# Mamba-2 SSD and a merged expert layer on one core: a split chunk output, a moved gated product and a reordered last step

## The chip, the cores and the metric

The kernel runs on one core of a Trainium2 chip. The metric is the device time of one execution in microseconds, lower being better. The core has five engines that run side by side, each with its own queue of instructions: TensorE (PE, matrix products into PSUM, with PEld for the loads of its stationary operand), VectorE (DVE), ScalarE (ACT), GpSimd (POOL) and SyncE (SP, which here issues DMAs). All data are float32.

## What is computed

Two stages follow one another. The first is the chunked state-space scan of Mamba-2, for 4 batches of 8 heads over 768 positions, with head size 32 and state size 16. The second is a layer of four experts (256 to 1024 to 256), all of which see every token, weighted by normalised domain probabilities.

```python
# stage 1, per chunk of positions: cum = cumsum(log a)
L = exp(cum[i] - cum[j]) * (i >= j)
y = ((C @ B.T) * L) @ x + (C @ state) * exp(cum)
state = exp(sum(log a)) * state + sum_j(B[j] x[j] * exp(cum[-1] - cum[j]))
# stage 2, tokens as rows of 8 heads x 32 = 256
p = domain_probs / (domain_probs.sum(-1, keepdims=True) + 1e-9)
out = sum_e p[:, e:e+1] * (maximum(x @ w1[e], 0) @ w2[e])
```

## The kernel before, in words

**Tiling.** The 3072 tokens are 24 chunks of 128, and these are 6 blocks (k) of 4 chunks (512 tokens, two halves b1 and b2 of 256). A block's chunks come from the four batches. Per block the second stage takes 8 steps (r), one for each expert e and each half jj of its hidden layer (512 of 1024 units); n counts the 48 steps. From step `PLAIN` = 2 on, each step does its first product (w1) and its second (w2) as seven products of half-size blocks, a Strassen scheme in Winograd's form; the sums of weights are made once by GpSimd (`sums_of`, L178) and kept in DRAM, the sums of activations by DVE (`sums`, `diff`) and in PSUM.

**Order of the work.** It is written out by hand (a manual schedule): the program text is the order of each engine's queue, and an engine waits only where an operand or a buffer isn't ready. The steps of the second stage of one block are interleaved with the first stage of the next block's chunks. Buffers are rotating pools; a tile waits until the readers of the tile that held its slot are done.

**First stage.** `spread` and `decay_part` make the decay factors LT by scans on DVE, `masks` makes the masked C (ACT), `scores` the products C B (PE), `masked` multiplies scores by LT (DVE, L396), and `outputs` (L408) makes y on PE (L430). y lies with the state's new part A in one PSUM tile of pool `ps_att` (tag "att", two buffers). ACT copies it to yT (L439) and A (L443, L444, L446).

**Second stage.** `fmul` (L477) makes the seven first products in two PSUM banks X and Y; `snap` (ACT, L498) copies bank X, `total` (DVE, L503) adds bank Y to a copy and gives z, `gated` (DVE, L513) takes max(z, 0) times the gate and gives h, and `diff` (DVE, L520) makes the sums T of h. `smul` (L561) makes the seven second products, one step later, into the PSUM tiles acc0 to acc3 (L576). The seven have the positions (1, 3, 7, 5, 6, 2, 4) in these: 1 and 3 in acc0, 7 and 5 in acc1, 6 and 2 in acc2, 4 in acc3. `plain_first` (L530) and `plain_second` are the ordinary products that the first two steps use.

**The start.** Chunks 0 to 3 are made one after another while there is no other work. `outputs([1])` (L716) is followed on PE by the first product of step 0 (`plain_first(0, 1, (0,))`, L540), which reads yT of chunks 0 and 1.

**A step with scores** (r = 3 and 6 in all blocks but the last, ten in all): after `gated(n, "21", "X")` comes `gated(n, "12", "z12")` (L847), then `smul(n - 1, 6)`, `scores` and the eight masked products (L853), then the T differences.

**The end.** For the first five blocks, `combine` and `turned_out` (a transpose on DVE in blocks of 32x32) prepare the result, and `leave` (L667) issues it from SP in pieces of 32 partitions, 16 KB each, over later steps. The last block has no later step: `finish` (L609) does the seven second products of the last step, the sums u and o, transposes on PE (L627), copies and three DMAs of 256, 128 and 128 KB (L651, L656, L658).

Of the kernel before, what the change touches and what calls it, by code (L numbers as in the profile page):

```python
# [8 lines left out]
FP32 = mybir.dt.float32  # L9
# [3 lines left out]
P = 128  # L13
NQ, NT = 4, 2
# [3 lines left out]
def kernel(  # L18
# [38 lines left out]
    nc = tc.nc  # L57

    NCH, _, W = xbc.shape
    E, DM, F = w1.shape  # L60
# [329 lines left out]
    def masked(cs, rs):  # L390
        for r in rs:
            for c in cs:
                q = r ^ 2 * turned_round(c)
                h = slice(NT * q, NT * q + NT)
                s = st[c]
                nc.vector.tensor_mul(s["MT"][:, h, 0:P], s["g"][q], s["LT"][:, h])  # L396
# [8 lines left out]

    state = {}

    def outputs(cs):  # L408

        ys = {}  # L410
# [119 lines left out]
    def plain_first(n, b, a=(0, 1)):  # L530

        k = n // SPB
        cols = slice(b * HB - HB, b * HB)
        f = first.setdefault(n, {})
        for bank, ws in [(("X", (A11, A12)), ("Y", (S3, A22)))[i] for i in a]:
            pool, tag = (ps_f, bank) if n or b > 1 else (ps_s, {"X": "acc2", "Y": "acc3"}[bank])
            f[bank] = pool.tile([P, JJ, HB], FP32, tag=tag, name=bank)
            for j in range(JJ):
                for i, w in enumerate(ws):
                    nc.tensor.matmul(  # L540
                        out=f[bank][:, j], lhsT=wt1[n][:, w, j * P:j * P + P],
                        rhs=yT[k][:, i, cols], start=(i == 0 and j == 0), stop=(i == 1),
                        skip_group_check=True)
# [39 lines left out]
    def keep(k, u):  # L583
        e = kept[k, u] = ffn.tile([P, 2, HB], FP32, tag=f"kept{u}", name=f"kept{u}", bufs=1)
        nc.scalar.copy(out=e, in_=acc[k, u])
# [23 lines left out]
    def finish(n):  # L609


        k = n // SPB
        add = nc.vector.tensor_add
        b1, b2 = slice(0, HB), slice(HB, BLK)
        o = ffn.tile([P, 2, BLK], FP32, tag="o", name="o", bufs=1)
        u = ffn.tile([P, 3, HB], FP32, tag="u", name="u", bufs=1)
        turned, rows = {}, {}

        def turn_out(b, d):
            if b not in turned:  # L620
                rows[b] = ffn.tile([P, 2, DM], FP32, tag="z", name="rows", bufs=3)
                turned[b] = [ps_f.tile([P, DM], FP32, tag=tag, name="turned") for tag in "XY"] \
                    if b == 0 else ps_att.tile([P, 2, DM], FP32, tag="att", name="turned")
            for i in range(2):
                lo = b * HB + i * P
                t = turned[b][i] if b == 0 else turned[b][:, i]
                nc.tensor.transpose(t[:, d * P:d * P + P], o[:, d, lo:lo + P], ident[:, 0])  # L627

        def dst(b):
            return out.rearrange("(i k p) m -> k p i m", k=NBLK, p=P)[k][:, 2 * b:2 * b + 2]  # L630

        smul(n, 1)
        smul(n, 3)
        keep(k, 0)
        p1, p3 = kept[k, 0][:, 0], kept[k, 0][:, 1]
        smul(n, 6)
        add(u[:, 0], acc[k, 2][:, 0], p1)
        add(u[:, 1], u[:, 0], p3)
        smul(n, 7)
        smul(n, 5)  # L640
        p7, p5 = acc[k, 1][:, 0], acc[k, 1][:, 1]
        add(u[:, 2], p7, u[:, 0])
        add(o[:, 1, b2], p5, u[:, 2])
        add(o[:, 0, b2], p5, u[:, 1])
        smul(n, 2)
        add(o[:, 0, b1], acc[k, 2][:, 1], p1)
        turn_out(1, 1)
        smul(n, 4)
        turn_out(1, 0)
        nc.scalar.copy(out=rows[1], in_=turned[1])  # L650
        nc.sync.dma_start(out=dst(1), in_=rows[1])  # L651
        turn_out(0, 0)
        add(o[:, 1, b1], acc[k, 3][:, 0], u[:, 2])
        turn_out(0, 1)
        nc.vector.tensor_copy(rows[0][:, 0], turned[0][0])
        nc.sync.dma_start(out=dst(0)[:, 0], in_=rows[0][:, 0])  # L656
        nc.scalar.copy(out=rows[0][:, 1], in_=turned[0][1])
        nc.scalar.dma_start(out=dst(0)[:, 1], in_=rows[0][:, 1])  # L658

    def turned_out(k):  # L660

# [2 lines left out]
        ot = kept[k, "ot"] = ffn.tile([P, 2, BLK // 32, 32], FP32, tag="ot", name="ot", bufs=1)  # L664
        nc.vector.transpose(ot.rearrange("p d b j -> p d (b j)"), o)

    def leave(k, c):  # L667

        dst = out.rearrange(
            "(c k b i) (d a j) -> c k a d i b j", k=NBLK, i=32, b=P // 32, j=32, d=2)[c, k]  # L670
        for q in range(P // 32):
            for d in range(2):
                nc.sync.dma_start(
                    out=dst[q, d],
                    in_=kept[k, "ot"][32 * q:32 * q + 32, d, P // 32 * c:P // 32 * (c + 1)])

    def opened(n):

# [34 lines left out]
    masked([1], (0, 1, 2))  # L713
    spread(2, ((ps_s, "acc2"), (ps_s, "acc3"), (ps_f, "Y"), (ps_s, "acc0")))
    masks(2)
    outputs([1])  # L716
    sum_w1(0, 0)
    load_decays(3)
    load_w2(1)
# [54 lines left out]
    for n in range(PLAIN, NS):  # L774
# [69 lines left out]
        total(n, 6, "12")  # L844
        fmul(n, 4)
        gated(n, "21", "X")
        gated(n, "12", "z12")  # L847
        if r == SPB - 1 and k < NBLK - 1:
            sums(k + 1)
        smul(n - 1, 6)  # L850
        if scored:
            scores(scored, ((ps_att, "att"), (ps_att, "att"), (ps_f, "Y"), (ps_f, "X")))
            masked(scored, (3, 2, 0, 1))  # L853
        smul(n - 1, 2)
        diff(n, "T3", "22", "12")
        smul(n - 1, 4)
# [60 lines left out]
```

## Time and profile before

| | |
|---|---|
| median of 4 runs | 639.97 us (639.66 to 640.31) |
| the profiled execution's own time | 640.31 us |
| its span, first to last instruction | 638.5 us |
| PE busy, its idle | 632.9 us (99%), 5.6 us |
| granted TensorE clock | 1.00 of full speed throughout |
| DVE, ACT, POOL busy | 483.8, 119.4, 109.8 us |
| chain that ended last | PE 98% of the span, DVE 1% |
| bytes moved by DMA | 121.61 MB, mean 190 GB/s |
| one second product (4 PE records) | 0.86 us |

In the timeline rows of the profile, the first column is the start in microseconds from the span's start, the second the duration; then come the engine, the source line, the operation, the tiles (output and inputs), and in brackets the idle time just ahead with what ended it. A fp32 matmul of 128x256 shows as two records; "x8" are eight records. The ends of matmuls are modelled: a record lasts some 0.2 us longer than the time until the next can start. Rows on PEld are loads of the stationary operand.

### The profile page before, as it was taken

Reading aid. Unit: us, or ns where it says so; the run is one execution under the profiler, and the core shown is the slowest. Engines: PE = TensorE matmul, PEld = TensorE weight load, DVE = VectorE, ACT = ScalarE, POOL = GpSimd, SP = SyncE. Lnnn points to the kernel's source line nnn. Section 1 sums busy time; section 2 is a strip of 40 time slices with the busy share of each in tenths; the row PEclk is TensorE's granted clock in tenths of the full one; section 3 lists DMA queues with packets and bytes.
Section 4 is the critical chain, followed back from the end, with each engine's and each line's share of the span. In section 5 each row is a group of like instructions: output and inputs, shape, how many; then the busy total and the mean of one; then the engine's idle time right before and its main releaser. Section 6 shows DMA issues by size and latency. Waiting matters only on the chain.

```text
span 638.5 us, 9231 instructions
## 1 busy us (share of the span) xinstructions
PE 632.9 (99%) x3407; PEld 537.3 (84%) x3407; DVE 483.8 (76%) x811; ACT 119.4 (19%) x259; POOL 109.8 (17%) x159
## 2 busy tenths in 40 slices
PE   9999999999999999999999999999999999999997
PEld 5788887888888888888888888888888888888886
DVE  7869989887777688778687778768877667756555
ACT  4011221212111221122211221212121211111110
POOL 5788557020001002000002000000100000100000
PEclk9999999999999999999999999999999999999999
DMA  7998894855766392667274676649365733156000
GB/s 226 304 313 288 258 327 179 285 187 166 180 207 240 79 377 62 236 187 243 96 285 152 172 195 190 235 129 332 102 203 166 254 142 132 63 173 218 1 1 33
DMA packets 97248, 121.61 MB, mean 190 GB/s; under 512 B 28840, under 2 KB 80436, under 8 KB 97204
## 3 DMA queue, kind: packets, MB, share of 16 engines
q1 hardware_dynamic: 94376, 111.20, 54.0%
q0 software_dynamic: 2304, 9.44, 3.7%
q8 instruction: 27, 0.44, 0.3%
q10 hardware_dynamic: 524, 0.39, 0.2%
q14 instruction: 17, 0.14, 0.1%
HBM read 108.16 MB, written 12.83 MB: 189 GB/s over the span
## 4 chain that ended last, share of the span: by engine, by line
PE 98%; DVE 1%; ACT 0%; issue 0%; DVEq 0%
PE acc L576 43%; PE X L491 25%; PE Y L491 19%; PE y L430 2%; PE acc L557 2%; PE g L384 2%; PE X L540 1%; PE Y L540 1%; PE y L418 1%; PE t L691 1%; PE a L322 0%; DVE hT L520 0%; DVE h L513 0%; DVE z L503 0%; PE gp L300 0%; PE turned L627 0%
## 5 line engine op out<-in xcount | busy, mean ns | idle before, releaser
L503 DVE TENSOR_TENSOR z<-Y,snap 128x512 f32<-128x512 f32 x138 | 94.6, 685 | 123.5 <-ACT snap L498 72.8
L576 PE MATMUL acc<-hT,wt 128*128 128x256 f32 x736 | 181.2, 379 | 0.0
L498 ACT COPY snap<-X 128x512 f32<-128x512 f32 x138 | 80.9, 586 | 464.5 <-PE X L491 388.0
L576 PEld LDWEIGHTS acc<-hT,wt 128*128 128x128 f32 x736 | 139.8, 190 | 19.0
L576 PE MATMUL acc<-h,wt 128*128 128x256 f32 x552 | 142.5, 381 | 0.0
L491 PE MATMUL X<-yS,wt 128*128 128x256 f32 x552 | 141.7, 379 | 0.0
L576 PEld LDWEIGHTS acc<-h,wt 128*128 128x128 f32 x552 | 104.1, 190 | 17.1 <-issue 2.0
L491 PEld LDWEIGHTS X<-yS,wt 128*128 128x128 f32 x552 | 104.8, 190 | 14.5 <-issue 0.3
L513 DVE SCALAR_TENSOR_TENSOR h<-z,gate 128x512 f32<-128x512 f32 x138 | 100.1, 726 | 3.5 <-PE acc L557 0.4
L491 PE MATMUL Y<-yT,wt 128*128 128x256 f32 x368 | 94.7, 380 | 0.1
L491 PEld LDWEIGHTS Y<-yT,wt 128*128 128x128 f32 x368 | 68.7, 190 | 11.3 <-DVE z L503 0.8
L520 DVE TENSOR_TENSOR hT<-h,hT 128x512 f32<-128x512 f32 x92 | 65.2, 709 | 1.8
L520 DVE TENSOR_TENSOR hT<-h,h 128x512 f32<-128x512 f32 x92 | 65.7, 755 | 1.1
L355 DVE TENSOR_TENSOR_SCAN LT<-ab,ident 128x512 f32<-128x512 f32 x42 | 52.1, 1242 | 0.0
L491 PE MATMUL Y<-yS,wt 128*128 128x256 f32 x184 | 48.3, 385 | 0.0
L491 PE MATMUL X<-yT,wt 128*128 128x256 f32 x184 | 47.2, 379 | 0.0
L360 POOL TENSOR_TENSOR MT<-xb,LT 128x128 f32<-128x128 f32 x20 | 8.6, 428 | 207.8 <-PE Y L491 68.8
L491 PEld LDWEIGHTS Y<-yS,wt 128*128 128x128 f32 x184 | 34.1, 190 | 6.4 <-issue 1.1
L491 PEld LDWEIGHTS X<-yT,wt 128*128 128x128 f32 x184 | 35.0, 190 | 4.8
L513 DVE SCALAR_TENSOR_TENSOR h<-X,gate 128x512 f32<-128x512 f32 x50 | 34.2, 685 | 6.0 <-PE X L491 3.4
L396 DVE TENSOR_TENSOR MT<-g,LT 128x256 f32<-128x256 f32 x94 | 32.4, 415 | 6.2 <-PE g L384 6.2
L341 POOL TENSOR_TENSOR cts<-ctm,dec 128x256 f32<-128x256 f32 x20 | 14.1, 724 | 129.1 <-DVE dec L338 129.1
(96 smaller groups left out, 321.9 us busy)
## 6 DMA issues: line engine op xcount, KB each, us to landing
wt<-in_w_dram SPq DMA_DIRECT2D x112, 256.0 KB
wt<-w_d SPq DMA_DIRECT2D x40, 640.0 KB
wt<-w_d SPq DMA_DIRECT2D x40, 512.0 KB
ab<-acut_d SPq DMA_DIRECT2D x21, 512.0 KB
gate<-p_d SPq DMA_DIRECT2D x23, 256.0 KB
w_d<-wt POOLq DMA_DIRECT2D x8, 640.0 KB, 3.8
wt<-in_w_dram SPq DMA_DIRECT2D x40, 128.0 KB
xb<-in_xbc_dram SPq DMA_DIRECT2D x14, 320.0 KB
```

Source lines behind the costliest of these rows:

```text
L341: nc.gpsimd.tensor_mul(cts, s["ctm"], dec.unsqueeze(1).to_broadcast([HN, NT, P]))
L355: nc.vector.tensor_tensor_scan(out=LT[:, i * w:i * w + w], data0=s["a"][i], data1=ident.rearrange("p h s -> p (h s)")[:, :w], initial=0.0, ...
L384: nc.tensor.matmul(out=g.rearrange("p t s -> p (t s)"), lhsT=s["xb"][k, OBT:OBT + P], rhs=s["ctm"][k].rearrange("p t s -> p (t s)"), start ...
L396: nc.vector.tensor_mul(s["MT"][:, h, 0:P], s["g"][q], s["LT"][:, h])
L430: nc.tensor.matmul(out=y[32 * q:32 * q + 32, t, 0:w], lhsT=s["xb"][:, h * D:h * D + D], rhs=s["MT"][:, NT * q + t, 0:w], start=(k == 0 and ...
L491: nc.tensor.matmul(out=f[bank][:, j], lhsT=wt1[n][:, w, j * P:j * P + P], rhs=rhs, start=(i in (1, 2, 5) and j == 0), stop=(j == JJ - 1), ...
L498: nc.scalar.copy(out=s, in_=first[n]["X"])
L503: nc.vector.tensor_add(z, first[n]["Y"], first[n][i])
L513: nc.vector.scalar_tensor_tensor(out=h, in0=first[n][src], scalar=0.0, in1=g.unsqueeze(1).to_broadcast([P, JJ, HB]), op0=ALU.max, op1=ALU. ...
L520: nc.vector.tensor_sub(h[o], h[x], h[y])
L540: nc.tensor.matmul(out=f[bank][:, j], lhsT=wt1[n][:, w, j * P:j * P + P], rhs=yT[k][:, i, cols], start=(i == 0 and j == 0), stop=(i == 1), ...
L576: nc.tensor.matmul(out=acc[k, u][:, half], lhsT=w2_op(n, w)[:, j], rhs=rhs[:, j], start=(begins and j == 0), stop=(n % SPB == SPB - 1 and ...
```

## The change

There are three parts. First, `outputs_apart` takes the place of `outputs` for chunk 1: its y is made in two PSUM tiles, one for each group t of four heads, and each is copied to yT by a copy of its own; A takes four copies instead of two. In `plain_first` the loops over the two input halves i and the two output halves j change places. Second, in steps with scores `gated(n, "12", "z12")` stands behind the masked products. Third, `finish` has the seven products in the order 1, 2, 6, 7, 4, 5, 3 and other sums; the first quarter of the result (d = 0, first half of the tokens) is transposed on DVE and leaves in eight pieces, in turn from SP and GpSimd; two quarters leave by a PE transpose, an ACT copy and a DMA of 128 KB from SP each; the last is transposed on PE in two buffers and leaves in two DMAs of 64 KB, from SP and ACT. `leave_part` is the body of `leave`, with the queue as an argument.

```diff
--- before.py
+++ after.py
@@ -404,6 +404,29 @@
         nc.gpsimd.tensor_mul(s["MT"][:, h, 0:P], g, s["LT"][:, h])
 
     state = {}
+
+    def outputs_apart(c):
+
+        s = st[c]
+        k, i = divmod(c, CPB)
+        s["A"] = att.tile([P, NT, N], FP32, tag="A", name="A", bufs=4)
+        ys = []
+        for t in range(NT):
+            y = ps_att.tile([P, P + N], FP32, tag="att", name="y")
+            ys.append(y)
+            for q in range(NQ):
+                h = NQ * t + q
+                nc.tensor.matmul(
+                    out=y[32 * q:32 * q + 32], lhsT=s["xb"][:, h * D:h * D + D],
+                    rhs=s["MT"][:, NT * q + t], start=True, stop=True,
+                    tile_position=(0, 32 * q), skip_group_check=True)
+            nc.scalar.copy(out=yT[k][:, t, i * P:i * P + P], in_=y[:, 0:P])
+        for t, y in enumerate(ys):
+            if i % 2:
+                nc.scalar.copy(out=s["A"][:HALF, t], in_=y[HALF:, P:])
+                nc.scalar.copy(out=s["A"][HALF:, t], in_=y[:HALF, P:])
+            else:
+                nc.scalar.copy(out=s["A"][:, t], in_=y[:, P:])
 
     def outputs(cs):
 
@@ -535,8 +558,8 @@
         for bank, ws in [(("X", (A11, A12)), ("Y", (S3, A22)))[i] for i in a]:
             pool, tag = (ps_f, bank) if n or b > 1 else (ps_s, {"X": "acc2", "Y": "acc3"}[bank])
             f[bank] = pool.tile([P, JJ, HB], FP32, tag=tag, name=bank)
-            for j in range(JJ):
-                for i, w in enumerate(ws):
+            for i, w in enumerate(ws):
+                for j in range(JJ):
                     nc.tensor.matmul(
                         out=f[bank][:, j], lhsT=wt1[n][:, w, j * P:j * P + P],
                         rhs=yT[k][:, i, cols], start=(i == 0 and j == 0), stop=(i == 1),
@@ -614,48 +637,51 @@
         b1, b2 = slice(0, HB), slice(HB, BLK)
         o = ffn.tile([P, 2, BLK], FP32, tag="o", name="o", bufs=1)
         u = ffn.tile([P, 3, HB], FP32, tag="u", name="u", bufs=1)
-        turned, rows = {}, {}
-
-        def turn_out(b, d):
-            if b not in turned:
-                rows[b] = ffn.tile([P, 2, DM], FP32, tag="z", name="rows", bufs=3)
-                turned[b] = [ps_f.tile([P, DM], FP32, tag=tag, name="turned") for tag in "XY"] \
-                    if b == 0 else ps_att.tile([P, 2, DM], FP32, tag="att", name="turned")
+        p1 = ffn.tile([P, 2, HB], FP32, tag="kept0", name="kept0", bufs=1)[:, 0]
+        ot = kept[k, "ot"] = ffn.tile([P, 2, BLK // 32, 32], FP32, tag="ot", name="ot", bufs=1)
+        dst = out.rearrange("(i k p) (d m) -> k d p i m", k=NBLK, p=P, d=2)[k]
+
+        def turn(d, b, i, t):
+            lo = b * HB + i * P
+            nc.tensor.transpose(t, o[:, d, lo:lo + P], ident[:, 0])
+
+        def quarter(d, b, pool, tag, queue):
+            rows = ffn.tile([P, 2, P], FP32, tag="z", name="rows", bufs=3)
+            t = pool.tile([P, 2, P], FP32, tag=tag, name="turned")
             for i in range(2):
-                lo = b * HB + i * P
-                t = turned[b][i] if b == 0 else turned[b][:, i]
-                nc.tensor.transpose(t[:, d * P:d * P + P], o[:, d, lo:lo + P], ident[:, 0])
-
-        def dst(b):
-            return out.rearrange("(i k p) m -> k p i m", k=NBLK, p=P)[k][:, 2 * b:2 * b + 2]
+                turn(d, b, i, t[:, i])
+            nc.scalar.copy(out=rows, in_=t)
+            queue.dma_start(out=dst[d][:, 2 * b:2 * b + 2], in_=rows)
 
         smul(n, 1)
-        smul(n, 3)
-        keep(k, 0)
-        p1, p3 = kept[k, 0][:, 0], kept[k, 0][:, 1]
+        nc.scalar.copy(out=p1, in_=acc[k, 0][:, 0])
+        smul(n, 2)
         smul(n, 6)
         add(u[:, 0], acc[k, 2][:, 0], p1)
-        add(u[:, 1], u[:, 0], p3)
+        add(o[:, 0, b1], acc[k, 2][:, 1], p1)
         smul(n, 7)
+        add(u[:, 1], acc[k, 1][:, 0], u[:, 0])
+        smul(n, 4)
+        w = HB // 32
+        nc.vector.transpose(ot[:, 0, :w].rearrange("p b j -> p (b j)"), o[:, 0, b1])
+        for c in range(2):
+            for q in range(P // 32):
+                leave_part(k, c, q, 0, (nc.sync, nc.gpsimd)[q % 2])
+        add(o[:, 1, b1], acc[k, 3][:, 0], u[:, 1])
         smul(n, 5)
-        p7, p5 = acc[k, 1][:, 0], acc[k, 1][:, 1]
-        add(u[:, 2], p7, u[:, 0])
-        add(o[:, 1, b2], p5, u[:, 2])
-        add(o[:, 0, b2], p5, u[:, 1])
-        smul(n, 2)
-        add(o[:, 0, b1], acc[k, 2][:, 1], p1)
-        turn_out(1, 1)
-        smul(n, 4)
-        turn_out(1, 0)
-        nc.scalar.copy(out=rows[1], in_=turned[1])
-        nc.sync.dma_start(out=dst(1), in_=rows[1])
-        turn_out(0, 0)
-        add(o[:, 1, b1], acc[k, 3][:, 0], u[:, 2])
-        turn_out(0, 1)
-        nc.vector.tensor_copy(rows[0][:, 0], turned[0][0])
-        nc.sync.dma_start(out=dst(0)[:, 0], in_=rows[0][:, 0])
-        nc.scalar.copy(out=rows[0][:, 1], in_=turned[0][1])
-        nc.scalar.dma_start(out=dst(0)[:, 1], in_=rows[0][:, 1])
+        add(o[:, 1, b2], acc[k, 1][:, 1], u[:, 1])
+        add(u[:, 2], acc[k, 1][:, 1], u[:, 0])
+        quarter(1, 0, ps_f, "X", nc.sync)
+        smul(n, 3)
+        quarter(1, 1, ps_f, "Y", nc.sync)
+        add(o[:, 0, b2], acc[k, 0][:, 1], u[:, 2])
+        rows = ffn.tile([P, 2, P], FP32, tag="z", name="rows", bufs=3)
+        for i, (copy, queue) in enumerate(
+                ((nc.vector.tensor_copy, nc.sync), (nc.scalar.copy, nc.scalar))):
+            t = ps_att.tile([P, P], FP32, tag="att", name="turned")
+            turn(0, 1, i, t)
+            copy(out=rows[:, i], in_=t)
+            queue.dma_start(out=dst[0][:, 2 + i], in_=rows[:, i])
 
     def turned_out(k):
 
@@ -664,15 +690,18 @@
         ot = kept[k, "ot"] = ffn.tile([P, 2, BLK // 32, 32], FP32, tag="ot", name="ot", bufs=1)
         nc.vector.transpose(ot.rearrange("p d b j -> p d (b j)"), o)
 
-    def leave(k, c):
-
+    def leave_part(k, c, q, d, queue):
         dst = out.rearrange(
             "(c k b i) (d a j) -> c k a d i b j", k=NBLK, i=32, b=P // 32, j=32, d=2)[c, k]
+        queue.dma_start(
+            out=dst[q, d],
+            in_=kept[k, "ot"][32 * q:32 * q + 32, d, P // 32 * c:P // 32 * (c + 1)])
+
+    def leave(k, c):
+
         for q in range(P // 32):
             for d in range(2):
-                nc.sync.dma_start(
-                    out=dst[q, d],
-                    in_=kept[k, "ot"][32 * q:32 * q + 32, d, P // 32 * c:P // 32 * (c + 1)])
+                leave_part(k, c, q, d, nc.sync)
 
     def opened(n):
 
@@ -713,7 +742,7 @@
     masked([1], (0, 1, 2))
     spread(2, ((ps_s, "acc2"), (ps_s, "acc3"), (ps_f, "Y"), (ps_s, "acc0")))
     masks(2)
-    outputs([1])
+    outputs_apart(1)
     sum_w1(0, 0)
     load_decays(3)
     load_w2(1)
@@ -844,13 +873,15 @@
         total(n, 6, "12")
         fmul(n, 4)
         gated(n, "21", "X")
-        gated(n, "12", "z12")
+        if not scored:
+            gated(n, "12", "z12")
         if r == SPB - 1 and k < NBLK - 1:
             sums(k + 1)
         smul(n - 1, 6)
         if scored:
             scores(scored, ((ps_att, "att"), (ps_att, "att"), (ps_f, "Y"), (ps_f, "X")))
             masked(scored, (3, 2, 0, 1))
+            gated(n, "12", "z12")
         smul(n - 1, 2)
         diff(n, "T3", "22", "12")
         smul(n - 1, 4)
```

## The prediction

> **What bounds the kernel now.** I read the page's busy shares first, then the waits of the matmul engine, then three stretches of the timeline where the change bites (12 to 14 us, 71 to 74 us and the last 5 us), and last the transfer rate of the closing microseconds.
>
> ```profile
> PE 632.9 (99%) x3407; PEld 537.3 (84%) x3407; DVE 483.8 (76%) x811; ACT 119.4 (19%) x259; POOL 109.8 (17%) x159
> ...
> PE X L540 <- ACT yT L439: 0.5, 1, 0.5
> ```
>
> PE is busy for 632.9 of 638.5 us. The other 5.6 us are about 1.1 before the first matmul, the 0.5 of the second line, small waits in the tail, and over 3.5 after the last transpose. So an edit pays only if it closes the 0.5, shortens the path behind the last matmul, or removes PE work. It costs if it makes PE wait in the middle, where it now hardly does.
>
> **Part 1: y of the second chunk in two banks, and the reordered `plain_first`.**
>
> ```profile
> 12.20 0.59 ACT L304 COPY gate<-gp 128x512 f32<-128x512 f32 x1 [0.61 <-PE gp L300]
> ...
> 12.68 0.69 ACT L369 ACTIVATE ctm<-xb,tmask 128x128 f32<-128x128 f32 x2
> ...
> 12.74 0.70 PE L430 MATMUL y<-MT,xb 128*32 128x144 f32 x16
> ...
> 13.50 0.37 ACT L439 COPY yT<-y 128x256 f32<-128x256 f32 x1
> ...
> 13.93 1.99 PE L540 MATMUL X<-yT,wt 128*128 128x256 f32 x8 [0.49 <-ACT yT L439]
> ```
>
> [...] PE idles 0.49 us ahead of the last line. After the change y's first half is complete half way through the y row, about 13.1. ACT is not free then: its two mask products end at 13.37. The row of 96x128 out of PSUM (L291) took 0.26 us against 0.37 for 128x256, and ACT copies here start about 0.1 before the one ahead ends. So the first half is copied from about 13.3 to 13.55. The reordered loop lets the first two matmuls of X (0.86 us) run on this half alone. The second copy, to about 13.8, hides behind them. X then starts near 13.6 instead of 13.93: **-0.34 us** (-0.2 if ACT doesn't overlap, -0.45 if the whole wait goes). Added are one yT copy and two copies of A (0.18 each); they push ACT's next masks from 14.29 to about 14.6, needed by PE only at 19.05. The extra PSUM buffer was last read by the gate copy, which ends at 12.79, before the second half of y starts. What is late next is the fourth scan of chunk 2 (it ends at 15.32), which frees the bank of the scores that PE starts at 15.85 less 0.34: 0.1 us of cover remains. The reordering moves no work: the same four weight loads and matmuls per bank.
>
> **Part 2: `gated(n, "12")` behind the masked products**, in the ten steps that have scores. The moved DVE instruction takes 0.68 us. In the later blocks it ended 0.68 us before the scores did, so the masked products start no sooner. DVE is instead 0.7 us later when it comes to the two T differences and to the next step's z. That z must be read out of bank Y before PE's next product into it: 170.81 against 174.08, over 3 us of cover, and DVE then idles 2.7 to 3.9 us. So eight steps cost nothing. In block 0 GpSimd's weight sums slow DVE's SBUF-to-SBUF work (that instruction 1.17 us, a T difference 1.28), and cover is thinnest one step after the first scores:
>
> ```profile
> 71.56 1.22 DVE L355 TENSOR_TENSOR_SCAN LT<-ab,ident 128x512 f32<-128x512 f32 x1
> ...
> 73.27 0.69 DVE L503 TENSOR_TENSOR z<-Y,snap 128x512 f32<-128x512 f32 x1 [0.49 <-ACT snap L498]
> 74.17 1.03 PE L491 MATMUL Y<-yT,wt 128*128 128x256 f32 x4
> ```
>
> DVE works without a break from 65.46 to 72.78, then idles 0.49. The moved instruction adds 0.7 to 1.2. Against that the gated product of 68.67 (1.19 us under GpSimd's sums, which end at 69.32) would start after them and take 0.69. Net +0.2 to +0.7 against the 0.49, and z has some 0.15 more before PE's matmul of 74.17 (a z that ended at 98.60 let PE start at 98.66). So PE waits 0 to 0.4 us here, once. One step later (107.81) DVE has 2.08 us of idle time. The gain side is zero, since the scores' end releases the masked products either way. I take **0**, range 0 to +0.4.
>
> **Part 3: the last step.** Columns as above; SPq and ACTq are DMA issues.
>
> ```profile
> 633.84 0.42 DVE L653 TENSOR_TENSOR o<-acc,u 128x256 f32<-128x256 f32 x1 [0.73 <-PE acc L576]
> ...
> 634.67 0.40 SPq L651 DMA_DIRECT2D out_dram<-rows  x1
> ...
> 634.79 0.37 ACT L657 COPY rows<-turned 128x256 f32<-128x256 f32 x1
> 635.16 0.41 SPq L656 DMA_DIRECT2D out_dram<-rows  x1
> 635.19 0.36 ACTq L658 DMA_DIRECT2D out_dram<-rows  x1
> ```
>
> Seven products of 0.865 us remain seven. By the rows' starts they run from 627.04; before, PE lost 0.28 us ahead of the first transposes, which waited for a chain of u and o sums. In the new order (1, 2, 6, 7, 4, 5, 3) every sum needed early follows a product that is early: products to 632.22; the sum for quarter (1,0) ends about 632.0 (product 4 is visible at 631.56, one add of 0.42), so its two transposes (0.27 apart from the next product) start without a wait. Product 3 runs 632.49 to 633.35. Quarter (1,1) is turned behind it, from 633.36 to 633.63, while DVE waits for product 3 (visible 0.2 later) and makes the last sum, 633.57 to 633.99. The last two transposes start at 634.05 and are readable at about 634.34 and 634.49. They lie in two buffers, so a 128x128 copy on DVE (about 0.29, from 0.42 for twice the columns) and one on ACT (0.26) follow: last issues at about 634.66 (SP) and **634.80** (ACT), against 635.19. That is -0.39. DVE's added transpose of 128x256 costs 0.31 (a quarter of the row of 1237 ns) in the gap before product 4 is ready; if it slipped behind, only quarter (1,0) would be late, by 0.3 at most.
>
> The larger share is the transfer:
>
> ```profile
> 635.50:636.00 0.50, 0.00 (x0) 0.00 (x0) 0.00 (x0) 0.00 (x0) 0.00 (x0) 1.00 0.80 262
> 636.00:636.50 0.50, 0.00 (x0) 0.00 (x0) 0.00 (x0) 0.00 (x0) 0.00 (x0) 1.00 1.05 356
> 636.50:637.00 0.50, 0.00 (x0) 0.00 (x0) 0.00 (x0) 0.00 (x0) 0.00 (x0) 1.00 1.03 338
> 637.00:637.50 0.50, 0.00 (x0) 0.00 (x0) 0.00 (x0) 0.00 (x0) 0.00 (x0) 1.00 0.28 92
> ```
>
> The last two columns are the DMA share and GB/s. All 512 KB leave in one burst, from about 635.55 (0.88 after the first issue) to 637.15, at the full rate; then 1.35 pass to the span's end. After the change 128 KB (eight pieces) are issued from about 631.4, 128 KB at about 633.3, 128 KB at 634.2 and 2 x 64 KB last. Only the last 256 KB are late: from 634.2 + 0.88 = 635.1 at 340 GB/s (0.77 us) to 635.9; the last issue's own data can't start before 635.68 and takes 0.2 to 0.4 (its runs are half as long, 512 B). Data ends at about 636.0, plus 1.35: 637.35. So the tail gives 638.5 - 637.35 = **-1.15 us**, of which 0.39 is the earlier last issue.
>
> Two rules of the Trainium skill speak against this. First, "DMA: Bandwidth & Descriptors", Rules for kernel authors, has small transfers coalesced, since under 64 KB one mostly pays overhead; each piece of `ot` is 16 KB in 128 B runs. In the trace the eight such issues of an earlier output took 3.67 us on SP (0.46 each, 144.34 to 148.01), while data moved at 30 to 44 GB/s. By the row four on SP end at 633.3, just as quarter (1,0) is ready, and cost nothing; paid on the path they would be 1.8 us. Second, "SBUF — State Buffer", SBUF: two separate sides, warns that a DMA issued from GpSimd has its descriptors written by GpSimd's cores, and waits while DVE holds the port they share. Here:
>
> ```profile
> L198 POOL DMA_DIRECT2D w_d<-wt x8: 571/574/597, 35.3 to 109.5; - x8
> ...
> DMA to landing us min/median/max: 3.3/6.3/9.2
> ```
>
> The issues took 0.57 us even beside DVE's two-input SBUF work, and the new sums mostly read PSUM. Four from 631.7 are issued by 634.1. Landing is the unknown: 3.3 to 9.2 us from the start, for 512 to 640 KB amid other traffic. Less 1.5 us for that size at the rate above, 16 KB land about 2 us after the last start at 633.5: 635.5, hidden. With the least measured, 3.3, it is 636.8, still hidden; with the median, 6.3, it is 639.8, past the old end. I take 2, nearest to the smallest row, and keep the far end for a rival.
>
> **Sum.** -0.34 + 0 - 1.15 = -1.49: span 637.0. The profiled run took 640.31, 1.81 beyond its span, and was the highest of the four; its own sum is 638.8. From the median of 639.97, **638.5 us**.
>
> **Rivals.**
> - *GpSimd's queue ends last (slower).* If its four small DMAs land 6 us or more after the last start, as the median did, the end is set at 639.8 plus up to 0.6 of closing work, less 0.34 for part 1: 640.1 in span, +1.6 us, 641.5. It decides from a landing of about 5 us on. For it: no GpSimd DMA here landed under 3.3 us, and none was issued for 500 us before. Against: the long landings fell in block 0, with busy DMA queues. 0.12.
> - *DVE becomes the bound in block 0.* The moved product makes PE wait 0.4 us around 74 and at the next such place, and part 1's lead is lost on DVE's unbroken chain of 46 to 59 us (beside GpSimd's sums, which run on their own clock). Then parts 1 and 2 cancel: -0.75 to -1.15, 639.0. For it: the 0.49 of slack. 0.22.
> - *The early leaving is hidden by a fixed cost*: the 1.35 us behind the last byte grows with many small writes, or the last quarters transfer more slowly. Tail -0.5, sum -0.8: 639.2. 0.10.
> - *As forecast*, 638.0 to 638.9. 0.56.
>
> **Chances.** 0.2% is 1.28 us, about what a measurement of this kernel can tell from no change, so the border is 638.69, close to my forecast. Faster: most of the forecast's 0.56, a little of the second: 0.50. Slower: 0.12. Within: 0.38. The range: 637.8 (the whole first wait gone, data over at 635.8) to 639.7 (both small rivals together); it leaves out the slow rival and a little below.
>
> **What would show it.** Right: the first X of `plain_first` starts near 13.6 with PE idle under 0.25; no wait of PE on z near 74 or 110; last ACT DMA issue near 634.5 (634.8 less 0.34); DMA share well below 1 in the last two microseconds before the data ends; 2.5 us from last issue to end instead of 3.3. Wrong: GpSimd's issues still landing after the last quarter; PE Y waiting for DVE in block 0; X still at 13.9.

## The result, and the profile after

| | before | after |
|---|---|---|
| median | 639.91 us (57 runs, 639.39 to 642.26) | 639.04 us (37 runs, 638.31 to 640.13) |
| ratio | 1 | 0.9983 [0.9979, 0.9988], about -1.1 us |
| profiled execution: own time, span | 640.31, 638.5 us | 638.92, 637.1 us |

The changed kernel is faster by 0.17% [0.12%, 0.21%], 0.8 to 1.3 us; 1.49 had been forecast. The border of 0.2% that the prediction names lies inside the interval, so whether it was crossed is open. The median of 639.04 is within the forecast's range and just above its likeliest band (638.0 to 638.9). In what follows line numbers are those of each kernel: `fmul` is L514 after (L491 before), `smul` L599 (L576), `plain_first` L563 (L540), `gated` L536 (L513).

On the page of the changed kernel PE is busy for 631.3 us, 1.6 us less than before. The records are not complete in either trace (3405 and 3407 of them), so this is no more than a hint. PE's wait ahead of the first X, whole execution (total, times, longest):

```profile
PE X L563 <- ACT yT L423: 0.2, 1, 0.2
```

It has fallen from 0.5 to 0.2. The timeline of the changed kernel at the three places that the prediction read (start, duration, engine, line, idle time ahead):

```profile
12.30 0.70 PE L419 MATMUL y<-MT,xb 128*32 128x144 f32 x16
...
12.85 0.49 ACT L423 COPY yT<-y 128x128 f32<-128x128 f32 x2
...
13.25 1.32 PE L563 MATMUL X<-yT,wt 128*128 128x256 f32 x5 [0.25 <-ACT yT L423]
...
19.35 1.23 DVE L355 TENSOR_TENSOR_SCAN LT<-ab,ident 128x512 f32<-128x512 f32 x1 [0.83 <-DMA ab<-acut_d]
...
72.79 0.69 DVE L526 TENSOR_TENSOR z<-Y,snap 128x512 f32<-128x512 f32 x1 [0.25 <-ACT snap L521]
...
73.70 1.03 PE L514 MATMUL Y<-yT,wt 128*128 128x256 f32 x4
...
633.88 0.29 DVE L683 COPY rows<-turned 128x128 f32<-128x128 f32 x1 [0.42 <-PE turned L646]
633.99 0.27 ACT L683 COPY rows<-turned 128x128 f32<-128x128 f32 x1 [0.37 <-PE turned L646]
634.20 0.35 SPq L684 DMA_DIRECT2D out_dram<-rows  x1
634.29 0.36 ACTq L684 DMA_DIRECT2D out_dram<-rows  x1
```

X follows the start of y by 0.95 us instead of 1.19. A new wait stands at 19.35: DVE waits 0.83 us for the decays of chunk 3. At 72.79 z has 0.25 us of idle time left of 0.49, and PE's Y follows without a wait. The last issue starts at 634.29 instead of 635.19. The stretches of the changed kernel's end; as before, the last two columns are the DMA share and GB/s:

```profile
633.50:634.00 0.50, 0.44 (x2) 0.20 (x2) 0.12 (x1) 0.13 (x2) 0.11 (x1) 1.00 0.41 110
634.00:634.50 0.50, 0.00 (x0) 0.00 (x0) 0.17 (x1) 0.26 (x1) 0.00 (x0) 1.00 0.73 202
634.50:635.00 0.50, 0.00 (x0) 0.00 (x0) 0.00 (x0) 0.00 (x0) 0.00 (x0) 1.00 0.90 257
635.00:635.50 0.50, 0.00 (x0) 0.00 (x0) 0.00 (x0) 0.00 (x0) 0.00 (x0) 1.00 0.89 257
635.50:636.00 0.50, 0.00 (x0) 0.00 (x0) 0.00 (x0) 0.00 (x0) 0.00 (x0) 0.90 0.11 31
```

Data now moves while the last product is still being turned, and is over at 635.56 instead of 637.14; but 1.54 us pass from there to the span's end, not 1.36, and the rate is 257 GB/s, not 338 to 356.

**A caution on the two spans.** y of chunk 1 starts at 12.74 us in the profile of before and at 12.30 after. Nothing that the change touches comes earlier. Over all thirteen profiles, one of each kernel, that start lies between 11.97 and 13.08, whether part 1 is in the kernel or not. So 0.44 of the 1.4 us between the two spans is scatter of the start, and each part is better measured from a mark inside the same execution. Three marks serve below: **y1**, the start of that y on PE; **M**, the start of the first of the three last products before the last step's seven (`acc<-hT`, 624.45 before, 623.98 after); and the end of the data, read in steps of 0.1 us. The spans are printed in steps of 0.1 us too, so the last two columns of the table can be off by 0.05.

| us | y1 | y1 to X | y1 to M | M to last issue | last issue to data end | data end to span end | M to span end |
|---|---|---|---|---|---|---|---|
| before | 12.74 | 1.19 | 611.71 | 10.74 | 1.95 | 1.36 | 14.05 |
| after | 12.30 | 0.95 | 611.68 | 10.31 | 1.27 | 1.54 | 13.12 |
| part 1 alone | 12.04 | 0.90 | 611.58 | 10.75 | 1.93 | 1.40 | 14.08 |
| part 2 alone | 12.11 | 1.19 | 611.72 | 10.75 | 1.94 | 1.38 | 14.07 |
| part 3 alone | 12.04 | 1.25 | 611.80 | 10.30 | 1.30 | 1.56 | 13.16 |
| parts 1 and 3 | 12.30 | 0.94 | 611.43 | 10.30 | 1.26 | 1.61 | 13.17 |
| all pieces from SP | 12.24 | 0.95 | 611.63 | 11.86 | 1.27 | 1.7 | 14.83 |
| quarters held | 11.97 | 0.90 | 611.57 | 10.71 | 1.84 | 1.51 | 14.06 |
| decays 3 early | 12.09 | 0.95 | 611.44 | 10.31 | 1.26 | 1.60 | 13.17 |
| loops as before | 12.19 | 0.95 | 611.46 | 10.30 | 1.29 | 1.56 | 13.15 |
| short runs | 12.43 | 1.19 | 612.07 | 10.74 | 2.21 | 1.45 | 14.40 |
| w2 later | 12.07 | 0.95 | 611.59 | 10.31 | 1.28 | 1.55 | 13.14 |
| first quarter by PE | 13.08 | 0.94 | 611.43 | 10.53 | 1.31 | 1.75 | 13.59 |

From before to after: -0.44 ahead of y1, -0.03 from there to M, -0.93 behind M. The sum is -1.40.

### The profile page after: what moved, and what is told of

It reads as the page before. It is cut to its first block, busy times and chain, and to the rows that moved or that the text cites. A ratio compares the mean times of both kernels' runs of the same rounds, so it can differ in the third digit from the quotient of the medians.

```text
span 637.1 us, 9254 instructions
## 1 busy us (share of the span) xinstructions
PE 631.3 (99%) x3405; PEld 536.8 (84%) x3405; DVE 481.7 (76%) x812; ACT 119.4 (19%) x263; POOL 111.8 (18%) x163
## 4 chain that ended last, share of the span: by engine, by line
PE 97%; DVE 1%; issue 0%; ACT 0%; POOL 0%; DVEq 0%; POOLq 0%
PE acc L599 43%; PE X L514 25%; PE Y L514 19%; PE acc L580 2%; PE y L453 2%; PE g L384 2%; PE X L563 1%; PE Y L563 1%; PE y L441 1%; PE t L720 0%; DVE hT L543 0%; DVE LT L355 0%; DVE h L536 0%; DVE z L526 0%; PE gp L300 0%
## 5 line engine op out<-in xcount | busy, mean ns | idle before, releaser
L599 PE MATMUL acc<-hT,wt 128*128 128x256 f32 x736 | 181.0, 379 | 0.0
L599 PEld LDWEIGHTS acc<-hT,wt 128*128 128x128 f32 x736 | 139.8, 190 | 19.0
L599 PE MATMUL acc<-h,wt 128*128 128x256 f32 x552 | 142.5, 381 | 0.0
L514 PE MATMUL X<-yS,wt 128*128 128x256 f32 x552 | 141.7, 379 | 0.0
L599 PEld LDWEIGHTS acc<-h,wt 128*128 128x128 f32 x552 | 104.0, 190 | 17.0 <-issue 2.3
L514 PEld LDWEIGHTS X<-yS,wt 128*128 128x128 f32 x552 | 104.8, 190 | 14.5 <-issue 0.3
L536 DVE SCALAR_TENSOR_TENSOR h<-z,gate 128x512 f32<-128x512 f32 x138 | 98.3, 712 | 3.5 <-PE acc L580 0.4
L514 PE MATMUL Y<-yT,wt 128*128 128x256 f32 x368 | 94.5, 379 | 0.1
L514 PEld LDWEIGHTS Y<-yT,wt 128*128 128x128 f32 x368 | 68.7, 190 | 11.1 <-DVE z L526 0.5
L543 DVE TENSOR_TENSOR hT<-h,h 128x512 f32<-128x512 f32 x92 | 64.2, 739 | 1.4
L514 PE MATMUL Y<-yS,wt 128*128 128x256 f32 x184 | 48.3, 385 | 0.0
L514 PE MATMUL X<-yT,wt 128*128 128x256 f32 x184 | 47.2, 379 | 0.0
L514 PEld LDWEIGHTS Y<-yS,wt 128*128 128x128 f32 x184 | 34.1, 190 | 6.4 <-issue 2.2
L514 PEld LDWEIGHTS X<-yT,wt 128*128 128x128 f32 x184 | 35.0, 190 | 4.8
L536 DVE SCALAR_TENSOR_TENSOR h<-X,gate 128x512 f32<-128x512 f32 x50 | 34.2, 684 | 5.9 <-PE X L514 3.6
```

The lines of the kernel that those rows point to most:

```text
L514: nc.tensor.matmul(out=f[bank][:, j], lhsT=wt1[n][:, w, j * P:j * P + P], rhs=rhs, start=(i in (1, 2, 5) and j == 0), stop=(j == JJ - 1), ...
L536: nc.vector.scalar_tensor_tensor(out=h, in0=first[n][src], scalar=0.0, in1=g.unsqueeze(1).to_broadcast([P, JJ, HB]), op0=ALU.max, op1=ALU. ...
L543: nc.vector.tensor_sub(h[o], h[x], h[y])
L599: nc.tensor.matmul(out=acc[k, u][:, half], lhsT=w2_op(n, w)[:, j], rhs=rhs[:, j], start=(begins and j == 0), stop=(n % SPB == SPB - 1 and ...
```

## The experiments

**One part at a time.** Three kernels have one part of the change each, and a fourth has parts 1 and 3.

```diff
-    outputs([1])                    # part 1 alone, with the new loops of plain_first
+    outputs_apart(1)
...
-        gated(n, "12", "z12")       # part 2 alone
...
             masked(scored, (3, 2, 0, 1))
+            gated(n, "12", "z12")
...
-        smul(n, 3)                  # part 3 alone: finish and leave_part as changed
-        keep(k, 0)
+        nc.scalar.copy(out=p1, in_=acc[k, 0][:, 0])
+        smul(n, 2)
```

> Only part 1 (y of chunk 1 in two banks, plain_first reordered), against the kernel before. Theory A (the forecast's sums hold): the first X of plain_first starts 0.25 to 0.34 us sooner after y's end and the lead reaches the end, so -0.25 to -0.35 us. Theory B (the lead is given back, because DVE waits for the decay factors of chunk 3, whose transfer runs on its own clock, so that y of chunk 3 waits): between 0 and -0.15 us, and a wait of DVE on ab at the start in the profile. Part 3 is absent, so the tail is as before (3.3 us from the last issue to the end).

> Only part 2 (gated 12 behind the masked products). Theory A: 0 within 0.15 us, since the z of the next step still leaves bank Y in time. Rival (DVE becomes the bound in block 0): PE waits for DVE's z near 74 us and the time is +0.2 to +0.4 us. The tail is as before.

> Only part 3 (order of the second products, quarters). Theory A: -1.15 us, 0.4 of it from the earlier last issue and 0.75 from the shorter drain. Rival C (the closing work behind the last byte grows): -0.7 to -0.9 us, with over 1.35 us from the last byte to the end of the span. GpSimd's pieces land within 2 us in both.

> The changed kernel without part 2. Theory A (part 2 costs nothing): as the changed kernel, -1.1 us. Rival (part 2 costs on DVE in block 0): -1.3 to -1.5 us, faster than the changed kernel. A third outcome: part 2 helps, then it is slower than the changed kernel, -0.9 or less.

| | ratio to before |
|---|---|
| part 1 alone | 0.9998 [0.9990, 1.0006] |
| part 2 alone | 0.9999 [0.9991, 1.0007] |
| part 3 alone | 0.9987 [0.9977, 0.9996] |
| parts 1 and 3 | 0.9984 [0.9977, 0.9990] |

Part 3 carries the gain, -0.8 us [-1.5, -0.3], and the table of marks says the same: M to the end falls from 14.05 to 13.16. That is less than theory A's 1.15, with a closing of 1.56, as rival C had it. Part 2 moves nothing. Part 1 brings X forward by 0.29 (0.90 for 1.19), but its time can't be told from none, and of the 0.29 only 0.13 is left at M. Theory B's reason is not what took the rest: in the profile of part 1 alone DVE doesn't wait for `ab`. The lead is whole until 54 us and loses 0.15 at 58 us (see "w2 later").

**All eight pieces from SP.** The changed kernel with the first quarter's pieces on one queue.

```diff
-                leave_part(k, c, q, 0, (nc.sync, nc.gpsimd)[q % 2])
+                leave_part(k, c, q, 0, nc.sync)
```

> The changed kernel with all eight early pieces issued from SP, none from GpSimd. Theory A (GpSimd's DMAs land in 1.7 to 2.0 us and are hidden): the two middle quarters are issued up to 1.6 us later on SP (eight pieces of 0.44 end at 634.6 instead of 632.9), more data is left for the end, so up to +0.4 us against the changed kernel. Theory C1 (a GpSimd DMA lengthens the closing work behind the last byte, which grew from 1.36 to 1.55 us): the closing falls back to about 1.36 us. Theory C2 (it grew for another reason, the shorter writes): it stays at 1.5 to 1.6 us.

It took 640.47 us, ratio to before 1.0008 [1.0001, 1.0016]: the whole gain is lost. That is 1.6 us above the changed kernel (1.71 behind M), where at most 0.4 had been expected. The DMA issues in its timeline:

```profile
630.99 3.65 SPq L696 DMA_DIRECT2D out_dram<-ot  x8
634.18 0.38 ACTq L684 DMA_DIRECT2D out_dram<-rows  x1
634.73 0.91 SPq L654 DMA_DIRECT2D out_dram<-rows  x2
635.73 0.44 SPq L684 DMA_DIRECT2D out_dram<-rows  x1
```

Eight issues hold SP for 3.65 us. The two middle quarters queue behind them and are issued from 634.73 instead of 632.93, and the last quarter's SP half behind those, at 635.73 instead of 634.20. What arrives late is thus not a piece but what is behind the pieces on the same queue; the expectation had left the last quarter out of that count. GpSimd's four in the changed kernel, by tile:

```profile
L696 POOL DMA_DIRECT2D out_dram<-ot x4: 548/554/612, 631.4 to 633.1; - x4
...
DMA to landing us min/median/max: 1.7/1.8/2.0
```

They land 2.0 us at most after their issue, by 635.1, ahead of the last data. The closing, 1.7 us, is no shorter without any output DMA on GpSimd: that queue is not what lengthens it.

**Quarters held.** The changed kernel, but the two middle quarters are issued behind the last one, from ACT and SP.

```diff
-            queue.dma_start(out=dst[d][:, 2 * b:2 * b + 2], in_=rows)
+            held.append((dst[d][:, 2 * b:2 * b + 2], rows))
...
+        for queue, (to, rows) in zip((nc.scalar, nc.sync), held):
+            queue.dma_start(out=to, in_=rows)
```

> The changed kernel, but the two middle quarters (128 KB each) are issued behind the last ones, on ACT and SP, so that 384 KB leave in one burst. Theory A (0.7 us of the tail's gain are the shorter drain): last issue +0.36 us, data over about 1.0 us later than in the changed kernel, +0.9 to +1.1 us in all. Rival (the time behind the last issue is a fixed cost and the bytes don't matter): +0.36 us.

639.55 us, ratio 0.9998 [0.9989, 1.0006]. Behind M it takes 14.06 us, as long as before the change and 0.94 more than the changed kernel, as theory A had it. Its last quarter is turned and issued at the same distance from M as in the changed kernel (SP at 633.76, ACT at 633.84, M at 623.54: 10.30). Behind it the held quarters put the last issue 0.40 later, and from there the data takes 0.57 longer (1.84 for 1.27). So the earlier last quarter is not enough: it pays only when the middle quarters have left ahead of it.

**Decays of chunk 3 early.** The changed kernel, with chunk 3's `ab` read from the input instead of the copy that the kernel writes. It leaves out the cut between the heads.

```diff
-            out=ab, in_=acut_d[real(c)].rearrange("h s -> (h s)").partition_broadcast(P))
+            out=ab, in_=(a if c == 3 else acut_d)[real(c)].rearrange("h s -> (h s)").partition_broadcast(P))
```

> The changed kernel, but the decay factors of chunk 3 are loaded from the input instead of from the cut copy in DRAM, so the load doesn't wait for that copy's store (it leaves out the cut between the heads, so chunk 3's masks are not those of the reference). Theory B (the lead of part 1 is partly given back to this transfer): DVE no longer waits on ab before chunk 3's scans, y of chunk 3 takes 0.63 us on PE, and the lead from the first X to the first second product stays whole; -0.1 to -0.4 us against the changed kernel. Theory A (it reaches the end anyway): no difference.

638.7 us, ratio 0.9981 [0.9973, 0.9989]. The load is issued at 11.65 us instead of 14.50. DVE's wait of 0.83 us is gone, and from X to the first product of `plain_second` it is 10.01 us instead of 10.41. The ratio can't be told from the changed kernel's.

**Loops as before.** The changed kernel with the old order of `plain_first`, one run.

```diff
-            for i, w in enumerate(ws):
-                for j in range(JJ):
+            for j in range(JJ):
+                for i, w in enumerate(ws):
```

> The changed kernel with the loops of plain_first in the old order. Theory: the third matmul row of X no longer hides the second copy; X's second matmul waits for the second half of yT, so PE loses about 0.2 us of the 0.25 to 0.29 that the two banks gave between y's start and the scores of chunk 2. If the reordering doesn't matter: the same 2.84 us from y's start to those scores as in the changed kernel.

X starts 0.95 us behind y1 and the scores follow 2.85 behind y1, against 0.95 and 2.84 with the new order. The reordering hides nothing that is not hidden already: ACT's two copies end 0.22 apart, so the second half is there when PE wants it in either order. The scores' row takes 0.87 us here instead of 0.71, but so it does with the new order in parts 1 and 3 (0.86): the loops are not the reason.

**w2 later.** The changed kernel, with the load of the first w2 moved from ahead of the constants to behind the loads of chunk 3's decays.

```diff
-    load_w2(0)
...
     load_decays(3)
+    load_w2(0)
```

> The changed kernel, with the load of the first w2 moved from ahead of the constants to behind the loads of chunk 3's decays, so that these have the queues more to themselves at the start. Theory B (part 1's lead is partly given back because DVE waits for the decays of chunk 3 to come in): no wait of DVE on ab ahead of the fourth scan, y of chunk 3 takes 0.63 to 0.70 us on PE instead of 1.09, and from the first X of plain_first to the first product of plain_second it is 10.0 instead of 10.4; the time is 0.1 to 0.4 us below the changed kernel. Rival (the decays come late because of their own way through DRAM, whatever else is in the queues): the wait on ab stays, time as the changed kernel's, or slower if the later w2 then makes the first second products wait.

638.52 us, ratio 0.9972 [0.9960, 0.9983], 6 runs. There is no wait on `ab`, and the first `plain_second` product is 10.01 us behind X, both as theory B said. But that the moved load did this is not shown: part 1 alone, quarters held and first quarter by PE have w2 where it was and don't wait either, and short runs waits 0.23 us without part 1. What the profiles do show is this. The load of `ab` was issued between 13.50 and 14.65 us (11.65 in decays 3 early). DVE waited in the five kernels where that was 1.84 us or more behind y1, and in none where it was 1.81 or less. Only the two longest waits reached PE: 0.83 in the changed kernel and 0.80 in all pieces from SP put the first `plain_second` product 0.3 to 0.4 us later.

The gain is not all kept. DVE and PE of this kernel at 58 us:

```profile
53.36 0.99 DVE L535 SCALAR_TENSOR_TENSOR h<-z,gate 128x512 f32<-128x512 f32 x1
54.28 2.34 DVE L542 TENSOR_TENSOR hT<-h,hT 128x512 f32<-128x512 f32 x2
...
56.78 0.58 DVE L483 TENSOR_TENSOR M<-S,qmask 128x128 f32<-128x128 f32 x1
57.28 0.68 DVE L525 TENSOR_TENSOR z<-Y,snap 128x512 f32<-128x512 f32 x1
...
56.08 1.89 PE L598 MATMUL acc<-hT,wt 128*128 128x256 f32 x8
58.02 1.13 PE L513 MATMUL Y<-yT,wt 128*128 128x256 f32 x4
```

and of the changed kernel:

```profile
53.39 0.69 DVE L536 SCALAR_TENSOR_TENSOR h<-z,gate 128x512 f32<-128x512 f32 x1
54.00 2.58 DVE L543 TENSOR_TENSOR hT<-h,hT 128x512 f32<-128x512 f32 x2
...
57.53 0.69 DVE L526 TENSOR_TENSOR z<-Y,snap 128x512 f32<-128x512 f32 x1 [0.22 <-ACT snap L521]
...
56.71 1.89 PE L599 MATMUL acc<-hT,wt 128*128 128x256 f32 x8
58.43 1.03 PE L514 MATMUL Y<-yT,wt 128*128 128x256 f32 x4
```

Eight records of `acc` take 1.72 us when nothing is late (56.71 to 58.43). With w2 later, z follows DVE's chain without a break, and PE's Y starts 1.94 behind: 0.22 lost. The same DVE instructions take different times in the two kernels: the two T differences ahead of these rows 3.12 us with w2 later and 2.29 in the changed kernel, h 0.99 and 0.69, the two differences behind it 2.34 and 2.58. For h the neighbour is plain: with w2 later GpSimd's sums run beside it (53.05 to 53.79, and on from 53.87), and in the changed kernel GpSimd is issuing a DMA (53.54 to 54.11).

When PE's rows are set against the same rows of before, the distance between the two kernels is constant from 30 to 54 us, and from 61 us it is what it is at M; between, it shifts. The shift is -0.16 in the four kernels with part 1 that had lost some of their lead by 24 us (after, parts 1 and 3, all pieces from SP, loops as before); +0.15 in three of the five that still had it whole (part 1 alone, quarters held, w2 later) and 0 in the other two (decays 3 early, first quarter by PE); 0 in parts 2 and 3 alone; and +0.34 in short runs, which has no part 1 at all. So it takes and gives 0.5 us from one profile to another. Each kernel has one profile, so whether the kernel or the single execution decides is not shown. The ratio of w2 later lies below that of the changed kernel, but the intervals overlap; it beats the kernel before, and that it beats the changed one is not shown.

**Short runs.** The kernel before, with its last two DMAs (of 128 KB each) in runs of 512 B instead of 1 KB; the copies and DMAs of these rows (not shown) take the same shape.

```diff
-                rows[b] = ffn.tile([P, 2, DM], FP32, tag="z", name="rows", bufs=3)
+                rows[b] = ffn.tile([P, 2, 2, P + 4], FP32, tag="ot", name="rows", bufs=1)[:, :, :, :P] \
+                    if b == 0 else ffn.tile([P, 2, DM], FP32, tag="z", name="rows", bufs=3)
```

> The kernel before, with one change: the last two DMAs (128 KB each, issued last from SP and ACT) read a padded tile, so that each row of 1 KB leaves as two runs of 512 B. Nothing else of the end is changed. Theory A (the runs of 512 B make the end of the changed kernel slower to transfer and slower to close): the time from the end of the data to the end of the span grows from 1.36 to about 1.55 us, the data share of the last 256 KB falls from about 340 to below 300 GB/s, last issue to data end 2.05 to 2.2 instead of 1.95; together +0.2 to +0.4 us. Rival (the closing grew for another reason, such as the number of DMAs or that two more of them come late on SP): closing 1.36, drain 1.95, time unchanged.

640.6 us, ratio 0.9999 [0.9983, 1.0016]: too wide to decide by time. Here is the stretch of its end in which the short runs move, behind the unchanged 256 KB, and below it one of the kernel before:

```profile
636.90:637.40 0.50, 0.00 (x0) 0.00 (x0) 0.00 (x0) 0.00 (x0) 0.00 (x0) 1.00 0.96 279
...
636.50:637.10 0.60, 0.00 (x0) 0.00 (x0) 0.00 (x0) 0.00 (x0) 0.00 (x0) 1.00 1.02 336
```

The short runs move at 279 GB/s, where before showed 336, and the way from last issue to data end grows by 0.26. At these rates 256 KB take 0.16 us longer. The issues are longer too, 0.64 and 0.66 us instead of 0.41 and 0.36, so the rate need not be the whole of the 0.26. Theory A holds for that half. For the closing it fails: 1.45, not 1.55.

**First quarter by PE.** The changed kernel, with the first quarter turned on PE and leaving in one DMA.

```diff
-        nc.vector.transpose(ot[:, 0, :w].rearrange("p b j -> p (b j)"), o[:, 0, b1])
-        for c in range(2):
-            for q in range(P // 32):
-                leave_part(k, c, q, 0, (nc.sync, nc.gpsimd)[q % 2])
+        quarter(0, 0, ps_att, "att", nc.sync)
```

> The changed kernel, with the first quarter (d = 0, first half of the tokens) leaving as the two middle ones do: two PE transposes, an ACT copy and one DMA of 128 KB from SP, in place of the DVE transpose and the eight pieces from SP and GpSimd. So the end has five DMAs instead of twelve. PE pays two more transposes behind product 4's queue place, 0.53 to 0.60 us by the other pairs. Theory A (the closing of the changed kernel is 0.2 us longer because of the eight small pieces): closing 1.36 to 1.40 instead of 1.54, so the time is 0.3 to 0.5 us above the changed kernel. Rival (the closing has another cause, or is only scatter): closing 1.5 to 1.6, the time 0.5 to 0.6 us above the changed kernel. In both the first quarter's way by DVE and small pieces is worth more than its closing costs.

639.89 us, ratio 0.9998 [0.9989, 1.0008]. Theory A falls: with five DMAs instead of twelve the closing is 1.75 us, the longest of all. The transposes cost less than expected, 0.22 us from M to the last issue (10.53 for 10.31). Together that is 0.47 behind M; the ratios, 0.9998 and 0.9983, stand for about 1 us. Much of the rest lies outside the span and so outside the marks: the runs of this kernel last 2.13 us beyond their spans (median), those of all others 1.77 to 1.83. Why is open.

**What the closing consists of.** The traces settle this. After its last issue SP takes one semaphore instruction after another before the program ends. Here is the last unbroken row of them in before, after and first quarter by PE (durations in ns, then the first and last start in us). Two later ones, some 0.61 and 0.06 us ahead of the end in all profiles, are left out:

```profile
L913 SPq EVENT_SEMAPHORE  x1: 28/28/28, 637.6 to 637.6; - x1
...
L944 SPq EVENT_SEMAPHORE  x5: 28/28/28, 636.0 to 636.3; - x5
...
L939 SPq EVENT_SEMAPHORE  x8: 28/28/28, 636.8 to 637.3; - x8
```

The first of each row is the one that waited for the last DMA of `rows`; it starts 0.36 to 0.37 us after the last packet in all thirteen profiles. Those behind it follow without a wait, 0.06 us apart. From the last of them it is 0.88 to 0.90 us to the end of the span everywhere. So the closing depends on how many of these instructions still stand behind the one for the DMA that lands last. Taken to the last packet (0.05 to 0.12 us later than the table's end of the data), it is:

| instructions behind | kernels | closing, us |
|---|---|---|
| 0 | before, part 1 alone, part 2 alone | 1.24 to 1.25 |
| 1 | short runs | 1.31 |
| 3 | quarters held | 1.44 |
| 4 | after, part 3 alone, parts 1 and 3, decays 3 early, loops as before, w2 later | 1.49 to 1.50 |
| 7 | all pieces from SP, first quarter by PE | 1.69 |

0.36 + 0.06 for each instruction behind + 0.89 gives every row within 0.02. No kernel was run that differs in this order alone, and what sets the order is not shown.

## Why the prediction was right, and where not

**Part 3, -1.15 forecast, -0.93 measured from M.** The mechanism was right; one term of the sum failed, the closing.
- *Earlier last issue*: forecast -0.39 (634.80 is 10.35 behind M), measured -0.43 (10.31). The transpose on DVE took 0.45 us instead of 0.31, but in a gap.
- *Shorter way from last issue to the data's end*: forecast -0.76 (1.95 to 1.2), measured -0.68 (1.27). The term was reckoned at 340 GB/s, the rate of 1 KB runs; the quarters leave in 512 B runs, at 257 on average and at 278 from 635.1 to 635.5 us. Quarters held shows that the gain hangs on the early leaving: without it M to the end is 14.06.
- *The closing, taken over unchanged at 1.35*: this step failed. It measured 1.54, and 1.51 to 1.75 in every kernel with the new last step, against 1.36 to 1.45 in those with the old one. The last issue is 2.81 us from the end, where 2.5 had been forecast. GpSimd's queue (all pieces from SP), the small pieces (first quarter by PE) and the short runs (short runs) are each ruled out as the whole cause. What the traces show instead is SP's chain of semaphore instructions: before, none stood behind the one for the last DMA; after, four do, and 4 times 0.06 is all but 0.02 of the growth, which is from 1.24 to 1.50 when taken to the last packet.

**Part 1, -0.34 forecast.** X started 0.24 to 0.29 earlier, not 0.34. PE still waits 0.25 for the first copy: it starts 0.55 behind y1 (12.85), and X 0.40 behind that. Of two terms that the working had in it, the reordered loops were worth nothing, since ACT's copies follow each other faster than PE's matmuls, and the four copies of A delayed nothing. Not in the working at all was DVE's wait for the decays of chunk 3, whose load is issued at its own time: in the profile of the changed kernel it takes 0.37 back. It comes and goes from profile to profile, with part 1 and without. In two others (parts 1 and 3, loops as before) 0.15 us goes at the scores of chunk 2 instead, where the prediction saw 0.1 us of cover. Behind all this stands the chain of DVE from 46 to 59 us, which the second rival named. It returned 0.16 here, and took 0.15 in three other kernels. At M, part 1 alone has 0.13 left, the changed kernel 0.03. The mean of the nine kernels with part 1 is 611.53 from y1 to M; before, part 2 alone and part 3 alone have 611.74 (611.83 with short runs). That is -0.2 to -0.3. The scatter is as large, but each of the nine lies below each of the four, the closest two by 0.03. This is the second of the mis-sized terms.

**Part 2, 0 forecast.** Right. z's idle time at 73 us fell from 0.49 to 0.25, a loss of cover of 0.24 at the lower end of the forecast 0.2 to 0.7, and no wait of PE followed. The wait ahead of Y near 98.5 us is the same as before (2.03 us from `acc` to Y, 2.04 before).

**The rivals.** *GpSimd's queue ends last*: refuted; the landing was 1.8 us, near the 2 that was taken, not the 6.3 of the median row. *DVE becomes the bound in block 0*: its figure of 639.0 is the one that was measured, but only half of its mechanism is seen. Part 1's lead is mostly lost, by the decays and the chain at 58 us, and part 2 costs nothing. *Hidden by a fixed cost*: a small share, +0.2 of the feared 0.65. The rule against small transfers in the Trainium skill, "DMA: Bandwidth & Descriptors", Rules for kernel authors, which the prediction weighed, would have been right on one queue: all pieces from SP is 1.6 us above the changed kernel. Split over two queues the pieces cost nothing ahead of the last issue (10.31 behind M, 10.35 forecast).

**The sum** of what was measured: -0.93 behind M and some -0.2 for part 1 make -1.1, the ratio's own value; the interval of 0.8 to 1.3 would allow part 1 anything from nothing to its forecast. The forecast span of 637.0 against 637.1 looks closer than it was: 0.44 of that agreement is the late start of the profile of before.

## What to carry to other kernels

At a kernel's end, ask how much of the output is still to move when the last product is done, and let the finished part leave while the matmul engine still works; but count every DMA issue by its queue, since eight issues of 0.46 us on the queue of the last transfer ate the whole gain. Look also at what the program still does behind the last byte: here an estimate of 0.24 us (4 times 0.06) would be saved if the DMA that lands last were also the last that SP looks at, which was not tried. A lead won at the start is worth only what the next arrival that doesn't move with it leaves over, so look past the wait removed for the next load and the next unbroken chain. Measure an edit from a mark inside the same execution when the start alone scatters by a microsecond.

## What the hardware showed that was not expected

- Writes to DRAM in runs of 512 B moved at 279 GB/s, in runs of 1 KB at 336, at the end of two kernels that differ in their last two DMAs alone. The Trainium skill, "DMA: Bandwidth & Descriptors", Specifications, puts the line rate at 512 B and above; here 512 B was a sixth short of the rate of 1 KB, and the measurement decides.
- A DMA of 16 KB issued from GpSimd at a quiet end took 0.55 us to issue and landed in 1.7 to 2.0 us from its start; amid the traffic of block 0, 512 to 640 KB took 3.3 to 9.2.
- The time from the last byte to the end of the span is not a constant: 1.24 to 1.69 us from the last packet, in steps of 0.06 us for each semaphore instruction that SP still has to take.
- The same PE row at 58 us was up to 0.5 us earlier or later against its neighbours. The DVE work ahead of it varied: the same `gated` instruction took 0.69 us in the changed kernel and 0.99 in w2 later, where a sum of GpSimd ran beside it. That such neighbours make all of the 0.5 is not shown.
